# Eighteen matmuls on zeros ahead of the first scores of a fused attention and MoE kernel

## The chip, the core and the metric

The kernel runs on one core of a Trainium2 chip. The metric is the device time of one execution in microseconds (us), as the median of the runs shown. Engines are called PE (TensorE's matmuls), PEld (TensorE's weight loads, which overlap PE), DVE (VectorE), ACT (ScalarE), POOL (GpSimd) and SP (the queue that issues most DMAs).

## The reference, cut to what matters

Three stages follow each other. The output of the first is the input of the second, and so on.

```python
scores = scale * np.matmul(q, k.transpose(0, 1, 3, 2))          # B 2, H 8, S 576, D 64, causal
cum    = np.cumsum(np.maximum(s, 0.0), axis=-1)
bias   = -(cum[:, :, :, None] - cum[:, :, None, :])
attn   = softmax(np.where(causal, -1e9, scores + np.minimum(bias, 0.0)))
x      = attn @ v                                               # 1152 tokens x 512
x      = sum(p[:, e:e+1] * (np.maximum(x @ w1[e], 0) @ w2[e]) for e in range(4))
out    = np.maximum(x @ w_in, 0)**2 @ w_out                     # d_ff 2048
```

The 18 matmuls of the change read a tile of zeros and write a PSUM bank that nothing reads, so they compute no part of this.

## The kernel before, in words

**Attention.** The work is cut into 16 + 24 + 40 steps: one step is one tile of queries of one head against all its keys. The loop at L683 is a software pipeline over the steps: in its round n the scores of step n are computed on PE (`do_qk`, L415), the row minima of step n-1 on DVE (`do_scores`, L449), the exponentials of step n-2 on ACT (`do_exp`, L472), the sums and the scaling of step n-3 on DVE and POOL (`do_sums`, L482; `do_norm`, L488), the transposes of step n-4 on PE (`do_transpose`, L501) and their copies out of PSUM on ACT (`do_pt`, L525). `do_pv` (L544) then multiplies by v on PE.

**The first 16 steps** are "plain" groups of two heads (L279). Their scores are three products in one PSUM tile: q times k in full float32 (L420) and two products (L430) that add the cumulative sums, with the rows of one head (64 of 128 partitions). They need q and k (loaded into `raw_p`, L323) and `cum_k`, `cum_q` (L612 to L618). From step 16 on the scores are two products with 128 rows (L439, L440), whose second operand is put together from a copy made by DMA (`tl<-th`, L363).

**Other work beside it.** The weights of the first expert are loaded (`w_load`, L88) and split into a high and a low part by ACT and DVE (`w_split`, L110, with the copy at L114 and the subtraction at L78) in the rounds of `SPLIT_AT`. The probabilities of the experts are normed by `p_norm` (L632 to L637), which the program writes in round 12. From round 21 on (`X_AT`), parts of the first expert's matmuls (L196, L222) fill PE between the steps; they use the PSUM pool `ph` of two banks.

**What sets the order.** SP's queue keeps the order of the program (L61). The order on PE, ACT, DVE and POOL is fixed when the program is built, by a planner that goes through a simulated timeline (L1156): an engine that would stand idle in that timeline takes what is ready, even if the program writes it later. `tc.issue_after` and `pin` hold single instructions back. On the chip each engine then works through its own list in that order.

**Behind the attention** come the remaining experts and the last stage (L935 and L953 above all), which fill most of the span.

Of the kernel before, what the change touches and what calls it, by code (L numbers as in the profile page):

```python
# [8 lines left out]
F32 = mybir.dt.float32  # L9
F32R = mybir.dt.float32r  # L10
# [6 lines left out]
P = 128  # L17
# [11 lines left out]
SPLIT_AT = [*range(0, 16, 2), *range(22, 38, 2)]  # L29
NP = 5  # L30
X_AT = 21, 45
KMAX = 512


# [12 lines left out]
def fused_kernel(ctx, tc, qk, v, s, dp, w1, w2, wi, wo, out):  # L47
# [5 lines left out]
    nc = tc.nc  # L53
# [131 lines left out]
    def ph_tile():  # L185
        pool = ph_pools[ph_count[0] % len(ph_pools)]
        ph_count[0] += 1
        return pool.tile([P, 512], F32, tag="ph", name="ph")
# [111 lines left out]
    with tc.tile_pool(name="att", bufs=2) as att, tc.tile_pool(name="atc", bufs=1) as const_a:  # L300
        aps = psum.enter_context(tc.tile_pool(name="aps", bufs=1, space=PSUM))

        mask = const_a.tile([P, KMAX + P], F32, name="mask")
        nc.gpsimd.memset(mask, 0.0)
        nc.gpsimd.affine_select(
            out=mask[:, KMAX:],
            in_=mask[:, KMAX:],
            pattern=[[-1, P]],
# [4 lines left out]
        )  # L313
        y_slots[:] = [ph_p]
        h_pools[:] = [att, 256, NF]
        st_pools[:] = [att, WBUF, "raw_w"]

        def qk_load(g):
# [16 lines left out]
        def bc_load(g):  # L335
            if g.plain:
                return
            r0 = g.b * H + g.heads[0]
            nc.sync.dma_start(out=g.th[AQ, : g.nq].bitcast(F32), in_=aug_d[0, r0, :, g.q0 : g.q1])
            nc.sync.dma_start(out=g.tl[AK, S : S + g.nk].bitcast(F32), in_=aug_d[1, r0, :, : g.nk])  # L340
# [13 lines left out]
        def qk_split(g):  # L354

            if g.plain:
                return []
            raw, th, tl = g.raw, g.th, g.tl
            q, k = slice(0, g.nq), slice(S, S + g.nk)

            def high_q():
                nc.scalar.copy(th[64:, q], raw[64:, q])
                nc.sync.dma_start(out=tl[:64, q].bitcast(F32), in_=th[64:, q].bitcast(F32))  # L363

            return [
                high_q,
                lambda: nc.scalar.copy(th[:, k], raw[:, k]),
                lambda: less(nc.vector, tl[64:, q], raw[64:, q], th[64:, q]),
                lambda: less(nc.gpsimd, tl[64:, k], raw[64:, k], th[64:, k]),
            ]  # L370
# [9 lines left out]
        def v_load(b, hp, nj):  # L380
            kt, full, half = v_parts(b, nj)
            t = att.tile([P, 5, 2 * D], F32, tag="v", name="v", bufs=2)
            c = slice(hp * 2 * D, (hp + 1) * 2 * D)
            nc.sync.dma_start(
                out=t[:, full[0] : full[-1] + 1, :],
                in_=v[b, kt[full[0]] : kt[full[-1] + 1], c].rearrange("(j p) c -> p j c", p=P),
            )
            for j in half:
                nc.sync.dma_start(out=t[:64, j, :], in_=v[b, kt[j] : kt[j + 1], c])
            vt[b, hp] = t  # L390
# [6 lines left out]
        for u in units:  # L397
            for i in u.tiles:
                t = Step()
# [8 lines left out]
        i = 0  # L408
# [6 lines left out]
        def do_qk(t):  # L415
            u, g = t.u, t.u.group
            if g.plain:
                ps = aps.tile([P, 512], F32, tag="s", name="s", bufs=3)
                rows = slice(u.slot * D, (u.slot + 1) * D)
                nc.tensor.matmul(  # L420
                    ps[: t.n, : t.w],
                    lhsT=g.raw[rows, t.q0 : t.q0 + t.n],
                    rhs=g.raw[rows, g.nq : g.nq + t.w],
                    start=True,
                    stop=False,
                )
                one = pick[rows, u.h // 2, :]
                sums = ((one[:, : t.n], cum_k[rows, : t.w]), (cum_q[rows, t.q0 : t.q0 + t.n], one[:, : t.w]))
                for i, (lhs, rhs) in enumerate(sums):
                    nc.tensor.matmul(ps[: t.n, : t.w], lhsT=lhs, rhs=rhs, start=False, stop=(i == 1))  # L430
                t.ps = [(ps, 0, t.w)]
                return
            q = slice(t.q0 - g.q0, t.q0 - g.q0 + t.n)
            t.ps = []
            cuts = [(0, t.w)] if t.w <= 512 else [(0, 288), (288, 576)]
            for a, z in cuts:
                ps = aps.tile([P, 512], F32, tag="s", name="s", bufs=3)
                k = slice(S + a, S + z)
                nc.tensor.matmul(ps[: t.n, : z - a], lhsT=g.tl[:, q], rhs=g.th[:, k], start=True, stop=False)  # L439
                t.mm = nc.tensor.matmul(  # L440
                    ps[: t.n, : z - a], lhsT=g.th[:, q], rhs=g.tl[:, k], start=False, stop=True
                )
                t.ps.append((ps, a, z))

        def do_bias(t):
            m0 = KMAX + t.n - t.w
            t.bias = mask[: t.n, m0 : KMAX + t.n]

# [33 lines left out]
        def do_sums(ts):  # L482
            t, c = ts[0], ts[0].c
            n, m = t.n, len(ts)
            nc.vector.tensor_scalar(t.st[:n, 4 + c : 4 + c + m], t.st[:n, 4 + c : 4 + c + m], 1e-9, None, op0=ALU.add)
            nc.vector.reciprocal(t.st[:n, 6 + c : 6 + c + m], t.st[:n, 4 + c : 4 + c + m])  # L486

        def do_norm(t):  # L488
            nc.gpsimd.tensor_scalar(  # L489
                t.p[: t.n, : t.w], t.p[: t.n, : t.w], t.st[: t.n, 6 + t.c : 7 + t.c], 1.0, op0=ALU.mult, op1=ALU.mult  # L490
            )
# [147 lines left out]
        def v_args(gi):  # L639
            g = groups[gi]  # L640
            return g.b, g.heads[0] // 2, 2 if gi < 4 else 5
# [8 lines left out]
        def w_ahead(n):  # L650
            while wloaded[0] < min(wdone[0] + n, len(PIECES)):
                w_load(0, *PIECES[wloaded[0]])
                wloaded[0] += 1
# [29 lines left out]
        for n in range(nsteps + 8):  # L683

            def step(i):
                return steps[i] if 0 <= i < nsteps else None

            cur, s1, s2, s3, s4, s5 = (step(n - i) for i in range(6))
            gi = group_first.get(n)
            if gi is not None:  # L690
                if gi + 1 < len(groups):
                    if gi > 0:
                        split_ops = qk_split(groups[gi + 1])
                        bc_load(groups[gi + 1])
                if gi > 0 and groups[gi].heads[0] % 2 == 0:
                    v_load(*v_args(gi))
            if s5 is not None:
                do_pt(s5)

            if s3 is not None and (s3.mate is None or s3.c == 1):  # L700
                ts = [s3] if s3.mate is None else [s3.mate, s3]
                do_sums(ts)
                for t in ts:
                    do_norm(t)

            if cur is not None:
                do_qk(cur)
            if pending_pv:
                x_next = pending_pv.pop(0)
                do_pv(x_next)  # L710
            if s4 is not None:
                do_transpose(s4)
            if s5 is not None and s5.last:
                u = s5.u
                if u.h % 2:
                    pending_pv.append(u)
                else:
                    pair[u.b, u.q0, u.h] = u

            if n + 1 < nsteps:  # L720
                do_bias(steps[n + 1])
            if s1 is not None:
                do_scores(s1)
            if s2 is not None:
                do_exp(s2)
            if x_next is not None:
                do_x(x_next)
            x_next = None
            nxt = min((i for i in group_first if i > n), default=n + 1) - n
            if gi is None:  # L730
                for _ in range(-(-len(split_ops) // nxt)):
                    split_ops.pop(0)()
            if n + 1 in group_first and 4 <= group_first[n + 1] + 2 < len(groups):
                qk_load(groups[group_first[n + 1] + 2])
            if n >= SPLIT_AT[0] - 4:
                w_ahead(WBUF)
            if n in SPLIT_AT:
                w_step()
            if n == 12:
                p_norm()  # L740
            if n == X_AT[0]:
                fill = fill_of((0, 256))
                rate = sum(c for _, c in fill) / (X_AT[1] - X_AT[0])
            elif n == X_AT[1]:
                fill += fill_of((256, 256))
                rate = sum(c for _, c in fill) / (nsteps + 2 - X_AT[1])
            owed += rate
            while fill and owed > 0:
                part, cost = fill.pop(0)
                with tc.issue_after(steps[min(n, nsteps - 1)].mm.ins):  # L750
                    part()
                owed -= cost
# [407 lines left out]
```

## Time and profile before

| | |
|---|---|
| runs shown | 718.12 us median of 3 (717.85, 718.12, 720.88) |
| the profiled execution | 719.2 us, its span 717.4 us |
| PE, PEld, DVE, ACT, POOL busy, share of the span | 96%, 83%, 71%, 49%, 43% |
| mean granted TensorE clock over the span | 0.996 |

The span goes from the first to the last instruction; the remaining 1.8 us lie around it. A matmul's busy time in the profile includes the time in which it drains, so matmuls that follow each other overlap in these rows, and the distance from one start to the next tells more than the length of one. "Granted clock" is a share of TensorE's full speed of 2.4 GHz: 1.00 is the upper of its two levels, 0.50 the lower.

### The profile page before, as it was taken

The page shows a single profiled execution, that of the slowest core. Times are in us where ns is not written, and L with a number is a line of the kernel's source. Part 1 is how long each engine was busy: PE and PEld are TensorE (multiplying, and loading weights), DVE is VectorE, ACT ScalarE, POOL GpSimd, SP SyncE. Part 2 cuts the span into 40 slices and gives each one's busy share as a digit, 9 for nine tenths or more (in the row PEclk, how much of TensorE's full clock was granted, in tenths as well). Part 3 has the DMA queues.
Part 4 walks back from the last instruction along what each step waited for, and adds up shares of the span by engine and source line. Part 5 has one row for each costly group of instructions (what it writes and reads, how often), then busy time and mean ns, then how long its engine had stood idle before and what let it go on. Part 6 is the DMA issues. An engine that isn't in the chain of part 4 may idle for free.

```text
span 717.4 us, 11852 instructions
## 1 busy us (share of the span) xinstructions
PE 689.6 (96%) x4100; PEld 598.5 (83%) x4100; DVE 507.6 (71%) x1145; ACT 353.1 (49%) x881; POOL 311.9 (43%) x332
## 2 busy tenths in 40 slices
PE   4999999999999999999999999999999999999997
PEld 3678788778998998989989989889997888899996
DVE  6668667762378548787787787869587788955463
ACT  4789767752254453443342534335474445535341
POOL 4446534431043675292580852822528625704000
PEclk9999999999999999999999999999999999999999
DMA  4554333200121234344242443441203232210012
GB/s 139 169 162 148 93 85 84 62 25 1 60 84 64 89 114 136 108 136 139 85 165 90 148 147 105 132 121 70 60 22 111 77 122 96 89 30 1 1 59 73
DMA packets 37179, 66.37 MB, mean 93 GB/s; under 512 B 4512, under 2 KB 12208, under 8 KB 37120
## 3 DMA queue, kind: packets, MB, share of 16 engines
q1 hardware_dynamic: 27904, 40.45, 18.7%
q10 hardware_dynamic: 9216, 25.17, 10.7%
q8 instruction: 32, 0.52, 0.3%
q14 instruction: 27, 0.22, 0.1%
HBM read 52.87 MB, written 10.90 MB: 89 GB/s over the span
## 4 chain that ended last, share of the span: by engine, by line
PE 74%; DVE 12%; ACT 4%; issue 4%; DMA 2%; POOL 2%; SPq 1%; ACTq 0%; DVEq 0%; POOLq 0%
PE y L953 26%; PE ph L935 17%; PE pc L935 7%; PE ph L196 7%; PE y L222 6%; PE o L560 4%; PE pt L512 3%; DVE dy L144 2%; PE s L439 2%; DVE raw_d L148 2%; PE s L440 1%; DVE raw_d L140 1%; ACT p L473 1%; POOL w L78 1%; DVE h L988 1%
## 5 line engine op out<-in xcount | busy, mean ns | idle before, releaser
L953 PE MATMUL y<-w,h 128*128 128x512 f32 x1080 | 276.7, 393 | 0.7 <-ACT h L993 0.7
L953 PEld LDWEIGHTS y<-w,h 128*128 128x128 f32 x1080 | 194.2, 188 | 32.0 <-ACT h L993 0.9
L935 PE MATMUL ph<-tx,w 128*128 128x256 f32 (+1 forms) x720 | 116.2, 297 | 0.1
L935 PEld LDWEIGHTS ph<-tx,w 128*128 128x128 f32 x720 | 106.9, 190 | 7.6 <-ACT u L976 0.9
L976 ACT COPY u<-ph 128x256 f32<-128x256 f32 (+1 forms) x120 | 47.7, 397 | 96.1 <-PE ph L935 93.9
L78 POOL TENSOR_TENSOR w<-raw_w,w 128x512 fp32r<-128x512 f32 x58 | 79.4, 1383 | 21.5 <-ACT w L902 21.5
L935 PE MATMUL pc<-xh,w 128*128 128x256 f32 (+1 forms) x320 | 78.2, 299 | 6.2 <-DVE r L992 2.8
L935 PE MATMUL ph<-xh,w 128*128 128x256 f32 (+1 forms) x320 | 78.3, 299 | 1.7 <-DVE h L988 1.2
L489 POOL TENSOR_SCALAR p<-p,stat 128x128 f32<-128x128 f32 (+8 forms) x80 | 46.8, 597 | 72.8 <-DVE stat L486 30.4
L78 POOL TENSOR_TENSOR w<-val,w 128x512 fp32r<-128x512 f32 x40 | 58.6, 1480 | 43.4 <-PE ph L196 41.7
L133 POOL TENSOR_SCALAR dy<-dy 128x512 f32<-128x512 f32 x32 | 20.0, 626 | 116.1 <-ACT dy L131 108.7
L935 PEld LDWEIGHTS pc<-xh,w 128*128 128x128 f32 x320 | 55.9, 188 | 10.4 <-DVE h L988 3.8
L935 PEld LDWEIGHTS ph<-xh,w 128*128 128x128 f32 x320 | 56.1, 189 | 5.1 <-DVE h L988 1.9
L473 ACT ACTIVATE p<-p,stat 128x128 f32<-128x128 f32 (+8 forms) x80 | 46.6, 583 | 23.7 <-DVE stat L459 20.3
L222 PE MATMUL y<-w,h 128*128 128x512 f32 x216 | 57.7, 396 | 0.0
L196 PE MATMUL ph<-xh,w 128*128 128x256 f32 (+1 forms) x256 | 57.3, 299 | 0.1
L459 DVE CUSTOM_DVE_ANT_0 p<-s,mask 128x128 f32<-128x128 f32 (+8 forms) x80 | 35.8, 451 | 17.7 <-PE pt L512 8.8
L935 PE MATMUL ph<-xl,w 128*128 128x256 f32 (+1 forms) x160 | 47.5, 297 | 0.0
L935 PE MATMUL pc<-xl,w 128*128 128x256 f32 (+1 forms) x160 | 47.3, 296 | 0.0
L994 DVE TENSOR_TENSOR h<-r,h 128x256 fp32r<-128x256 f32 (+1 forms) x64 | 36.2, 571 | 13.7 <-ACT h L993 12.5
L196 PEld LDWEIGHTS ph<-xh,w 128*128 128x128 f32 x256 | 43.1, 188 | 1.5 <-DVE h L210 0.4
L222 PEld LDWEIGHTS y<-w,h 128*128 128x128 f32 x216 | 38.7, 188 | 6.2 <-DVE stat L459 0.3
(135 smaller groups left out, 1272.7 us busy)
## 6 DMA issues: line engine op xcount, KB each, us to landing
raw_w<-in_w SPq DMA_DIRECT2D x64, 256.0 KB
raw_d<-in_wi ACTq DMA_DIRECT2D x16, 512.0 KB
staged<-dy ACTq DMA_DIRECT2D x32, 256.0 KB
raw_d<-in_wo ACTq DMA_DIRECT2D x16, 512.0 KB
raw_w<-staged SPq DMA_DIRECT2D x32, 256.0 KB
raw<-in_qk SPq DMA_DIRECT2D x40, 144.0 KB
v<-in_v SPq DMA_DIRECT2D x8, 256.0 KB
out<-acc_a SPq DMA_DIRECT2D x6, 256.0 KB
```

Source lines behind the costliest of these rows:

```text
L78: eng.tensor_tensor(out_, a, b.bitcast(F32), op=ALU.subtract)
L196: nc.tensor.matmul(ps[:, :n], lhsT=w1_ap(e, wh, kk, f), rhs=x[:, kk, t0 : t0 + n], start=(i == 0), stop=(i == 3 * KD - 1),)
L222: mm = nc.tensor.matmul(ps, lhsT=h[:, hh, o : o + P], rhs=w2_ap(e, wh, f), start=(f == 0 and i == 0), stop=(f == NF - 1 and i == 2),)
L459: nc.vector.tensor_tensor_reduce(t.p[: t.n, a:z], ps[: t.n, : z - a], t.bias[:, a:z], scale=-0.125, scalar=init, op0=ALU.add, op1=ALU.min, ...
L473: nc.scalar.activation(t.p[: t.n, : t.w], t.p[: t.n, : t.w], AF.Exp, bias=t.nmax, scale=-1.0, accum_out=t.st[: t.n, 4 + t.c : 5 + t.c],)
L489: nc.gpsimd.tensor_scalar(t.p[: t.n, : t.w], t.p[: t.n, : t.w], t.st[: t.n, 6 + t.c : 7 + t.c], 1.0, op0=ALU.mult, op1=ALU.mult)
L512: nc.tensor.transpose(tp_ap(t, j), t.p[: t.n, kt[j] : kt[j + 1]], ident[: t.n, : t.n])
L560: return nc.tensor.matmul(u.o[i * D : (i + 1) * D, qs - u.q0 : u.nq], lhsT=vv[:kn, j, i * D : (i + 1) * D], rhs=rhs, start=(j == 0), stop= ...
L935: nc.tensor.matmul(ps[:, :n], lhsT=pw[q][s][:, wh, c : c + P], rhs=x_part(b, xn, xx, k2), start=(first and m == 0), stop=(m == 5), skip_gr ...
L953: nc.tensor.matmul(ps, lhsT=hs[j][:, hh, o : o + P], rhs=wt[e, 2, g][:, wh, j * DM : (j + 1) * DM], start=(g % 2 == 0 and i == 0 and j == ...
L976: nc.scalar.copy(t[:, :n], ps[:, :n])
L994: nc.vector.tensor_tensor(lo, r, hi.bitcast(F32), op=ALU.subtract)
```

## The change

A tile of zeros is set by DVE, one tile of the pool `ph` is taken and never read, and 18 matmuls of 128 rows, 128 columns of weights and 512 columns of data, all zeros, write it. They stand in the program ahead of the attention's loads and steps. `WARM` also has places for more such matmuls behind the scores of the first rounds; with its last number 0 none is issued there.

```diff
+WARM = 18, 0, 0
...
         h_pools[:] = [att, 256, NF]
+        zeros = const_a.tile([P, 512], F32R, name="zeros")
+        nc.vector.memset(zeros.bitcast(F32), 0.0)
+
+        def keep_warm(after, n):
+            with tc.issue_after(after) if after is not None else nullcontext():
+                for _ in range(n):
+                    nc.tensor.matmul(idle, lhsT=zeros[:, :P], rhs=zeros, start=True, stop=True)
+
+        idle = ph_tile()
+        keep_warm(None, WARM[0])
         st_pools[:] = [att, WBUF, "raw_w"]
...
-                    nc.tensor.matmul(ps[: t.n, : t.w], lhsT=lhs, rhs=rhs, start=False, stop=(i == 1))
+                    t.mm = nc.tensor.matmul(ps[: t.n, : t.w], lhsT=lhs, rhs=rhs, start=False, stop=(i == 1))
...
             if cur is not None:
                 do_qk(cur)
+                if n < WARM[2]:
+                    keep_warm(cur.mm.ins, WARM[1])
```

## Rows read from the trace of the kernel before

**Rows 1.** Busy us of each engine by stretch, then granted clock, DMA share, GB/s
```profile
12.65:34.30 21.65, 20.77 (x83) 14.63 (x83) 15.40 (x54) 16.60 (x53) 9.66 (x14) 1.00 0.57 168
...
12.65:43.80 31.15, 28.09 (x111) 19.25 (x111) 21.57 (x76) 23.45 (x72) 12.84 (x20) 1.00 0.54 162
...
46.60:60.00 13.40, 13.40 (x106) 12.08 (x106) 10.48 (x37) 12.41 (x32) 9.76 (x10) 1.00 0.61 181
```

**Rows 2.** PE by shape, 8 to 36.2 us: count, busy us, mean ns, idle before
```profile
L512 PE MATMUL pt<-ident,p 128*128 128x128 f32 x18 | 6.1, 443 | 0.6 <-ACT ptk L536 0.5
```

**Rows 3.** The same view, 43 to 110 us
```profile
L512 PE MATMUL pt<-ident,p 128*128 128x128 f32 x68 | 11.3, 276 | 1.0 <-POOL p L489 1.0
```

**Rows 4.** PE in order of time, 36 to 45 us: start, length, instruction
```profile
36.30 0.66 PE L439 MATMUL s<-th,tl 128*128 128x384 f32 x1 [1.06 <-DMA tl<-th]
...
37.07 0.63 PE L439 MATMUL s<-th,tl 128*128 128x512 f32 x1
37.50 0.63 PE L440 MATMUL s<-tl,th 128*128 128x512 f32 x1
...
41.20 0.94 PE L512 MATMUL pt<-ident,p 128*128 128x128 f32 x3
43.10 0.55 PE L512 MATMUL pt<-ident,p 128*128 128x128 f32 x3 [0.96 <-POOL p L489]
...
44.28 0.39 PE L439 MATMUL s<-th,tl 128*128 128x512 f32 x1
44.51 0.40 PE L440 MATMUL s<-tl,th 128*128 128x512 f32 x1
```

**Rows 5.** PE in order of time, 538 to 562 us
```profile
541.59 1.04 PE L935 MATMUL ph<-tx,w 128*128 128x320 f32 x6
...
545.52 0.42 PE L935 MATMUL pc<-xh,w 128*128 128x320 f32 x1 [1.23 <-DVE u L983]
...
547.05 0.41 PE L935 MATMUL ph<-xh,w 128*128 128x320 f32 x1 [0.38 <-DVE r L992]
...
548.36 1.80 PE L935 MATMUL ph<-tx,w 128*128 128x320 f32 x6
```

**Rows 6.** Busy us by stretches of 1 us, as in rows 1
```profile
548.00:549.00 1.00, 1.00 (x6) 1.00 (x5) 0.69 (x2) 1.00 (x3) 0.56 (x1) 0.50 0.79 266
...
551.00:552.00 1.00, 1.00 (x7) 0.83 (x6) 0.87 (x3) 0.65 (x2) 1.00 (x2) 0.98 0.61 84
```

**Rows 7.** PE in order of time, 463 to 476 us
```profile
471.48 0.39 PE L935 MATMUL ph<-xh,w 128*128 128x256 f32 x1 [1.18 <-DVE h L988]
```

**Rows 8.** Busy us by stretches of 5 us, as in rows 1
```profile
470.00:475.00 5.00, 3.82 (x21) 3.05 (x20) 4.02 (x9) 1.45 (x4) 0.08 (x1) 1.00 0.39 122
```

**Rows 9.** All engines in order of time, 0 to 16 us
```profile
0.79 0.06 DVE L63 MEMSET warm<- 1x1 f32 x1 [0.79 <-PEq L1150]
0.86 0.64 POOL L304 MEMSET mask<- 128x640 f32 x1
...
2.53 1.02 DVE L593 TENSOR_SCALAR sc<-sc 16x320 f32<-16x320 f32 x1 [1.69 <-DMA sc<-in_s]
...
7.85 1.65 PE L420 MATMUL s<-raw_p 64*128 64x128 f32 x6 [7.85 <-DMA raw_p<-in_qk]
...
9.61 0.78 PE L430 MATMUL s<-w,cum_q 64*128 64x128 f32 x3
10.24 0.75 DVE L628 TENSOR_SCALAR aug<-aug 16x1152 fp32r<-16x1152 f32 x1
...
12.17 0.19 DVE L634 TENSOR_REDUCE psum__364<-praw 128x9 f32<-128x36 f32 x1 [1.18 <-DMA praw<-in_dp]
12.30 0.29 DVE L459 CUSTOM_DVE_ANT_0 p<-s,mask 128x128 f32<-128x128 f32 x1
...
12.65 1.22 PE L420 MATMUL s<-raw_p 64*128 64x256 f32 x3 [2.25 <-DVE stat L459]
...
15.31 0.60 ACT L114 CAST w<-raw_w 128x512 fp32r<-128x512 f32 x1
...
15.95 0.69 DVE L78 TENSOR_TENSOR w<-raw_w,w 128x512 fp32r<-128x512 f32 x1
```

## The prediction, made before the result was known

> **What bounds the kernel now.** I read the busy times by stretch first. From 46.6 us on PE is the bound: it is busy 13.40 us of 13.40 right there [rows 1]. PE's later work is the same before and after, so whatever the change is worth must come from PE's reaching that state earlier or later. Its place is the start, up to about 44 us.
>
> Second, the same shapes at two places. In the first stage a transpose of 128x128 takes 443 ns [rows 2], later 276 ns [rows 3]; two matmuls of 512 columns start 0.43 us apart at 37.07 us, and 0.23 us apart at 44.28 us [rows 4]. So TensorE runs at its lower level (1.2 GHz) up to some 42 us and at the upper (2.4 GHz) from 43.10 us, where three transposes take 0.55 us instead of 0.94 [rows 4]. The granted-clock column says 1.00 for the early stretches too [rows 1]; there the lengths contradict it, and I go by the lengths. The clock rose after PE had worked without a gap since 36.30 us [rows 4]. It had not risen before, though PE was busy 20.77 us of the 21.65 between 12.65 and 34.3 [rows 1].
>
> Third, the start in order of time [rows 9]. PE does nothing until q and k land at 7.85 us. Its first scores are done at 9.61 + 0.78 = 10.39 us. They then wait: DVE finishes L628 at 10.99, stands in front of the norming of probabilities (L634) until their load lands, and takes the first scores at 12.30. PE's next scores, released by that, start at 12.65 after 2.25 us of idleness.
>
> **The zeros' tile.** DVE's new memset has 128x512 elements. The nearest price is POOL's memset of 128x640, 0.64 us; in the same proportion 0.51, and DVE's 0.69 us for a 128x512 subtraction is the upper end [rows 9]. DVE is idle from 0.85 to 2.53 us for a load, so it costs nothing there. Without that cover it would cost its 0.5 to 0.7 us. PE can then start at about 0.85 + 0.6 = 1.45 us. No DMA is added, and SP, ACT and POOL get no new instruction. The unread bank belongs to a pool that the program uses only from round 21 on; until then no one waits for it.
>
> **The eighteen matmuls.** All at the lower level: 18 x 0.43 = 7.74 us [rows 4], with some 0.2 us for the last to drain, and so an end at 1.45 + 7.94 = 9.39 us, 1.54 us behind the landing of q and k. If the clock rises on the way, they end earlier: all at the upper level is 18 x 0.23 = 4.14 us and an end at 5.8 us. These are the two ends. PE's own record of a rise is the one after 36.30 us, within about 6 us of steady work [rows 4]; at 548.36 us the lower level gave way within 3 us of dense work [rows 5, 6]. Either puts the rise inside the burst, so I take an end between 7 and 8.8 us.
>
> **What the first scores gain or lose.** They take 10.39 - 7.85 = 2.54 us at the lower level. In the worst case they start at 9.24, when the last zeros have streamed, and end at 11.8 us. In the best they start at 7.85 and take 0.23/0.43 of that, 1.4 us, to end at 9.2 us. Both lie ahead of 12.30 us, where DVE takes them. So 0 us on the path, with 0.5 us left in the worst case; what covers them is DVE's wait for the probabilities. If that wait were gone, DVE could take them at 10.99: the worst case would then cost 0.8 us against a start at that time, and the best nothing.
>
> **Is the clock still up at 12.65?** This decides. The trace shows one fall: PE stood idle 1.23 us, did six matmuls, stood 0.38 us, and then the granted clock was 0.50 from 548 to 551 us; six matmuls that had taken 1.04 us took 1.80 [rows 5, 6]. It shows a hold as well: after 1.18 us of idleness at 470 us, with dense work on both sides, the clock stayed at 1.00 [rows 7, 8]. In the changed kernel there lies between the zeros' end and 12.65 us a wait of at least 2.25 us [rows 9], up to 3.4 if the scores run fast (12.65 - 9.2), and beside it only scores on half the rows. That is more idleness than the fall had, and less work around it. I take it that the clock is at 1.2 GHz again at about 12.65 us. From there to 42 us the stage is that of before, and of that the trace says that its work, even with PE 96% busy, doesn't raise the clock [rows 1]. Gain: 0 us; if the clock outlasts the gap by 2 us or so, the scores and transposes up to 15 us gain at most half of that, 1 us.
>
> **Sum.** 0 (memset) + 0 (first scores) + 0 (clock, 0 to -1) = 0 on a profiled execution of 719.2 us (span 717.4 and 1.8 around it). That execution lies 1.1 us above the median of the runs, 718.1 us, to which the forecast is tied: 718.0 us.
>
> **Rival 1, faster: the clock stays up through the first stage.** For it: a hold over 1.18 us of idleness is in the trace [rows 7, 8], and PE is the fullest engine from 12.65 to 43.80 us, 28.09 of 31.15 us, so the stage would shorten [rows 1]. Against it: the one fall had a shorter wait than the one here [rows 5, 6]. Price: at full clock PE needs 28.09 x 0.23/0.43 = 15 us, so ACT with 23.45 us becomes the bound; at the share that ACT reaches in the next stage, 12.41/13.40 = 0.93, the stage takes 25.3 us instead of 31.15: -5.8 us, 712.2 us. The waits for DMA copies that stay would take part of it back; 2 us is the low end. The Trainium skill, TensorE: Matmul & The Clock Gate, section "Why this matters for your kernels", advises to issue matmuls ahead of the timed work, and puts the fall down to idle gaps longer than the 2.25 us here. By that rule the clock would hold at 10.39 to 12.65 us, and this rival would be the forecast. The trace's fall after 1.23 us doesn't agree with it.
>
> **Rival 2, slower: the planner turns the order on DVE.** The zeros stand ahead of the scores in the planner's timeline too, which makes DVE seem idle longer. It fills such holes with later work: the norming that the program writes in round 12 already stands ahead of the first scores [rows 9]. If one subtraction of a split weight (L78) came ahead of L459 as well, DVE would wait for the weights and ACT's copy: L78 ran from 15.95 to 16.64 us, so the first scores would be taken at 16.64 instead of 12.30 [rows 9]. Price +4.3 us, 722.4 us, less what the later steps catch up (ACT is busy only 16.60 of 21.65 us there [rows 1]), so +2 to +4.3. It decides from the first split that is placed there. Against it: the weights' loads stand behind those of the probabilities on SP, so the planner should see them late as well.
>
> **Rival 3: the zeros don't raise the clock at all.** No row shows a burst on zeros. The burst then takes 7.74 us, the first scores end at 11.8 us and are still covered: 718.1 us. In time this can't be told from the forecast.
>
> **How the numbers follow.** Forecast (rise, then fall before or soon after 12.65) 0.52, rival 3 0.15, rival 1 0.17, rival 2 0.16. About 0.5%, 3.6 us, is what a measurement of this kernel can tell from no change; the three runs of before span 3 us. Rival 1's price lies beyond it for most of its bounds, as does rival 2's at its full price; a shorter rival 2 counts as no change, and in return a plan that is turned in another place can also cost. So faster 0.17, same 0.67, slower 0.16. The range holds both cases without change with their scatter up to 720.9, rival 1 down to two thirds of its price (718.0 - 4 = 714.0) and rival 2 up to 721.8, short of its full price. Left out are the ends of both rivals, together under 0.2.
>
> **What the changed profile would show.** The zeros on PE from about 1.5 us, first 0.43 us apart and then 0.23. The first scores between 7.85 and 9.3 us; L459 at about 12.3. Transposes between 12.65 and 42 us of about 443 ns again, and three transposes of 0.55 us only behind some 43 us. I am wrong if the transposes at 13 to 30 us take 276 ns (rival 1), if a subtraction L78 stands ahead of the first L459 on DVE (rival 2), or if PE's first gap-free work of L196 starts more than 2 us away from 46.6 us.

## The result, and the profile after

Behind the change the median is 723.32 us (20 runs, 720.59 to 726.25), beside 718.35 us for the kernel before (20 runs, 715.49 to 720.93): ratio 1.0069, 95% interval 1.0052 to 1.0085. It is slower by 5 us, where 718.0 was forecast. A second set of runs (e6 below) gave 1.0042 [1.0022, 1.0062]. The profiled execution is the quickest of its 20: 720.59 us, span 718.8, mean clock 0.979; so its trace shows less of the loss than the median does. Its lines are those of before plus 1 near the top and plus 13 further down: L420, L459, L512 and L196 are now L433, L472, L525 and L197.

The start, all engines in order of time, of the kernel after (start, length, instruction, in brackets the idle time before it and what ended it):

```profile
0.94 0.48 DVE L318 MEMSET zeros<- 128x512 f32 x1
...
1.48 6.20 PE L325 MATMUL ph<-zeros 128*128 128x512 f32 x18 [1.48 <-DVE zeros L318]
...
7.83 0.92 PE L433 MATMUL s<-raw_p 64*128 64x128 f32 x6 [0.17 <-DMA raw_p<-in_qk]
...
9.11 0.49 PE L443 MATMUL s<-w,cum_q 64*128 64x128 f32 x3
...
11.88 0.19 DVE L647 TENSOR_REDUCE psum__385<-praw 128x9 f32<-128x36 f32 x1 [1.39 <-DMA praw<-in_dp]
12.11 0.17 DVE L648 TENSOR_SCALAR psum__385<-psum__385 128x9 f32<-128x9 f32 x1
12.31 0.22 DVE L649 RECIPROCAL psum__385<-psum__385 128x9 f32<-128x9 f32 x1
12.44 0.29 DVE L472 CUSTOM_DVE_ANT_0 p<-s,mask 128x128 f32<-128x128 f32 x1
...
12.80 0.79 PE L433 MATMUL s<-raw_p 64*128 64x256 f32 x1 [3.19 <-DVE stat L472]
```

Against [rows 9]: the first scores are done at 9.60 instead of 10.39 us, DVE takes them at 12.44 instead of 12.30, and PE's wait grows from 2.25 to 3.19 us. So the zeros have bought idle time here and nothing else. The busy times by stretch (columns as in [rows 1]) show what the clock did with that:

```profile
5.40:7.70 2.30, 2.27 (x10) 1.50 (x8) 1.77 (x4) 1.54 (x3) 1.27 (x3) 1.00 0.71 189
...
12.65:34.30 21.65, 21.20 (x83) 15.62 (x84) 11.90 (x52) 15.87 (x51) 8.83 (x16) 0.50 0.49 158
12.65:43.80 31.15, 28.04 (x108) 20.00 (x108) 18.60 (x74) 22.26 (x70) 11.09 (x19) 0.51 0.49 153
46.60:60.00 13.40, 13.35 (x103) 11.86 (x103) 12.02 (x39) 12.38 (x31) 8.46 (x10) 1.00 0.60 177
```

The upper level comes inside the burst, at 5.39 us, and is gone at 12.22, in PE's wait. From there to 42.94 us the column reads 0.50, with transposes of 446 ns as before [rows 2]; behind 43 us they take 278 ns [rows 3]:

```profile
L525 PE MATMUL pt<-ident,p 128*128 128x128 f32 x16 | 5.5, 446 | 0.0
...
L525 PE MATMUL pt<-ident,p 128*128 128x128 f32 x68 | 11.0, 278 | 0.8 <-POOL p L502 0.4 <-ACT ptk L549 0.3
```

All that is as forecast. But look at DVE in the stretch to 34.30: 11.90 us of work where it had 15.40 [rows 1]. DVE does other work there. **The order has changed.** SP's queue is the same; the lists of PE, DVE and ACT differ from those of before in some 50 places each, POOL's in a few. The first difference is on DVE at 12.11 us: two more instructions of the norming (L648, L649, shown above) stand ahead of the first row minimum, where before one stood [rows 9]. On PE it begins at about 15 us (two more sets of scores ahead of the first transposes). In the trace the last differences are at about 125 us on PE and 130 us on DVE; behind them nothing differs. Two places show what it does. PE near 37 us, in order of time:

```profile
36.94 0.66 PE L452 MATMUL s<-th,tl 128*128 128x384 f32 x1 [2.03 <-DMA tl<-th]
37.40 0.53 PE L453 MATMUL s<-tl,th 128*128 128x384 f32 x1
37.72 0.63 PE L452 MATMUL s<-th,tl 128*128 128x512 f32 x1
38.14 0.63 PE L453 MATMUL s<-tl,th 128*128 128x512 f32 x1
38.57 0.45 PE L452 MATMUL s<-th,tl 128*64 128x288 f32 x1
38.81 0.45 PE L453 MATMUL s<-tl,th 128*64 128x288 f32 x1
39.05 0.84 PE L525 MATMUL pt<-ident,p 128*128 128x128 f32 x3
```

Before, the wait for the copy `tl<-th` was 1.06 us [rows 4], and behind two sets of scores came a transpose. In the kernel before, PE's next two lines are:

```profile
37.93 0.41 PE L512 MATMUL pt<-ident,p 128*128 128x128 f32 x1
37.99 0.59 PE L439 MATMUL s<-th,tl 128*64 128x288 f32 x1
```

Now three transposes stand behind three sets of scores and a longer wait; the scores themselves begin 0.64 us later. And PE near 131 us, in the kernel after:

```profile
128.74 0.86 PE L223 MATMUL y<-w,h 128*128 128x512 f32 x3
131.33 0.63 PE L525 MATMUL pt<-ident,p 128*64 128x128 f32 x4 [1.73 <-POOL p L502]
```

The same instruction in the kernel before:

```profile
129.33 0.62 PE L512 MATMUL pt<-ident,p 128*64 128x128 f32 x4 [0.65 <-POOL p L489]
```

That is 1.08 us more of waiting. The order on DVE just ahead of it points to where it comes from. DVE and POOL in the kernel after:

```profile
127.74 1.45 DVE L79 TENSOR_TENSOR tl<-raw,th 64x576 fp32r<-64x576 f32 x1 [0.48 <-ACT th L375]
...
129.61 0.47 DVE L472 CUSTOM_DVE_ANT_0 p<-s,mask 128x320 f32<-128x320 f32 x1
...
130.01 0.15 DVE L499 RECIPROCAL stat<-stat 64x1 f32<-64x1 f32 x1
...
130.36 2.55 POOL L502 TENSOR_SCALAR p<-p,stat 64x64 f32<-64x64 f32 x5 [1.79 <-DVE stat L498]
```

In the kernel before:

```profile
126.15 1.33 DVE L78 TENSOR_TENSOR tl<-raw,th 64x576 fp32r<-64x576 f32 x1
...
128.00 0.15 DVE L486 RECIPROCAL stat<-stat 64x1 f32<-64x1 f32 x1
...
128.36 1.64 POOL L489 TENSOR_SCALAR p<-p,stat 64x64 f32<-64x64 f32 x3 [1.50 <-DVE stat L485]
128.38 0.49 DVE L459 CUSTOM_DVE_ANT_0 p<-s,mask 128x320 f32<-128x320 f32 x1
```

In the new order DVE's subtraction waits 0.48 us for ACT's cast, and a row minimum of 0.47 us stands ahead of the reciprocal that POOL's scaling needs. Together that is most of the 1.08 us; neither was tried alone.

The row minimum of step 16 comes 2.41 us later than before (39.83 against 37.42), the first L197 1.38 us (48.04 against 46.66), and L950 begins 2.08 us later (212.46 against L935's 210.39). At the end of the spans 1.4 us are left of that. The order behind is the same, but the clock is not: in the execution of before it was at the lower level from 547.62 to 551.03 us as well, in that of after it wasn't.

### The profile page after: what moved, and what is told of

Its sections match the earlier page's. It is cut to its first block, busy times and chain, and to the rows that moved or that the text cites. A ratio compares the mean times of both kernels' runs of the same rounds, so it can differ in the third digit from the quotient of the medians.

```text
span 718.8 us, 11889 instructions
## 1 busy us (share of the span) xinstructions
PE 694.5 (97%) x4118; PEld 602.1 (84%) x4118; DVE 504.7 (70%) x1146; ACT 353.0 (49%) x881; POOL 310.4 (43%) x332
## 4 chain that ended last, share of the span: by engine, by line
PE 76%; DVE 12%; issue 4%; ACT 3%; POOL 2%; SPq 1%; DMA 1%; ACTq 1%; DVEq 0%; POOLq 0%
PE y L968 26%; PE ph L950 16%; PE pc L950 7%; PE ph L197 7%; PE y L223 6%; PE o L573 4%; PE pt L525 4%; DVE dy L145 2%; PE s L452 2%; DVE raw_d L149 2%; PE s L453 1%; DVE raw_d L141 1%; PE s L433 1%; POOL w L79 1%; DVE h L1003 1%
## 5 line engine op out<-in xcount | busy, mean ns | idle before, releaser
L950 PE MATMUL ph<-tx,w 128*128 128x256 f32 (+1 forms) x720 | 115.5, 296 | 0.1
L950 PEld LDWEIGHTS ph<-tx,w 128*128 128x128 f32 x720 | 106.2, 189 | 7.5 <-ACT u L991 0.9
L79 POOL TENSOR_TENSOR w<-raw_w,w 128x512 fp32r<-128x512 f32 x58 | 80.2, 1398 | 20.2 <-ACT w L917 20.2
L950 PE MATMUL pc<-xh,w 128*128 128x256 f32 (+1 forms) x320 | 78.4, 299 | 6.6 <-DVE r L1007 3.1
L950 PE MATMUL ph<-xh,w 128*128 128x256 f32 (+1 forms) x320 | 78.0, 298 | 1.7 <-DVE h L1003 0.8
L79 POOL TENSOR_TENSOR w<-val,w 128x512 fp32r<-128x512 f32 x40 | 58.6, 1480 | 43.6 <-ACT w L910 43.6
L502 POOL TENSOR_SCALAR p<-p,stat 128x128 f32<-128x128 f32 (+8 forms) x80 | 45.3, 580 | 69.6 <-DVE stat L499 42.6
L950 PEld LDWEIGHTS pc<-xh,w 128*128 128x128 f32 x320 | 56.0, 188 | 11.2 <-DVE r L1007 4.4
L950 PEld LDWEIGHTS ph<-xh,w 128*128 128x128 f32 x320 | 56.0, 188 | 5.1 <-DVE h L1003 1.5
L197 PE MATMUL ph<-xh,w 128*128 128x256 f32 (+1 forms) x256 | 58.0, 301 | 0.1
L472 DVE CUSTOM_DVE_ANT_0 p<-s,mask 128x128 f32<-128x128 f32 (+8 forms) x80 | 35.6, 452 | 25.2 <-PE pt L525 20.2
L950 PE MATMUL ph<-xl,w 128*128 128x256 f32 (+1 forms) x160 | 47.4, 296 | 0.0
L950 PE MATMUL pc<-xl,w 128*128 128x256 f32 (+1 forms) x160 | 47.4, 296 | 0.0
L197 PEld LDWEIGHTS ph<-xh,w 128*128 128x128 f32 x256 | 43.1, 188 | 1.4 <-DVE h L211 0.4
```

The source lines that it names most:

```text
L79: eng.tensor_tensor(out_, a, b.bitcast(F32), op=ALU.subtract)
L197: nc.tensor.matmul(ps[:, :n], lhsT=w1_ap(e, wh, kk, f), rhs=x[:, kk, t0 : t0 + n], start=(i == 0), stop=(i == 3 * KD - 1),)
L472: nc.vector.tensor_tensor_reduce(t.p[: t.n, a:z], ps[: t.n, : z - a], t.bias[:, a:z], scale=-0.125, scalar=init, op0=ALU.add, op1=ALU.min, ...
L502: nc.gpsimd.tensor_scalar(t.p[: t.n, : t.w], t.p[: t.n, : t.w], t.st[: t.n, 6 + t.c : 7 + t.c], 1.0, op0=ALU.mult, op1=ALU.mult)
L950: nc.tensor.matmul(ps[:, :n], lhsT=pw[q][s][:, wh, c : c + P], rhs=x_part(b, xn, xx, k2), start=(first and m == 0), stop=(m == 5), skip_gr ...
```

## The experiments

Medians of the kernel before in these sets: 720.11 us for e1 to e4, 719.04 for e5 to e8, 719.11 for e9 to e12, 719.51 for e13 to e16. Every kernel here computes the whole result; zeros and order are all that differs.

**First question: the clock and the zeros, or the order?** One to ten zeros leave the order on every engine as before; from 11 on the planner gives another, and 11, 15 and 18 each give their own.

e1, ten zeros:

```diff
-WARM = 18, 0, 0
+WARM = 10, 0, 0
```

> Ten zeros instead of eighteen. All engines keep the order of the kernel before; only the memset and the ten matmuls are new. Theory P (the new order of instructions that the planner makes in the attention costs the time): as before, ratio 0.998 to 1.002, about 718.3 us. Theory C (the clock's early rise and fall costs the time, by a later second rise): the clock rises at about 5 us here too and falls again before 13, so +3 to +5 us, ratio 1.004 to 1.007.

717.84 us against 720.11: ratio 0.9977 [0.9958, 0.9996]. With the order of before, ten zeros do no harm. Stretches of its profile (columns as in [rows 1]):

```profile
34.30:37.00 2.70, 2.70 (x10) 2.10 (x10) 2.00 (x11) 1.70 (x7) 0.97 (x3) 0.50 0.74 225
37.10:46.60 9.50, 7.29 (x56) 5.23 (x54) 7.31 (x25) 8.69 (x24) 5.24 (x7) 1.00 0.56 162
```

Its second rise came at 37.05 us, where the kernel before had it at 42.45, and its L197 began 1.77 us earlier than before. But its row minimum of step 16 came at 36.23 us, 1.20 us early, and that is ahead of the rise. The last section says how far executions scatter here.

e2 has 11 zeros (`WARM = 11, 0, 0`), the first number that turns the order:

> Eleven zeros: one more than the run with ten, but the planner now orders PE, ACT, DVE and POOL in another way from the first steps on. P: it has a time of its own, over 2 us away from the run with ten, to either side. C: the same as the run with ten within 1 us, since 0.2 to 0.4 us of zeros more change nothing in the clock.

719.51 us, 1.0000 [0.9982, 1.0018]: 1.7 us above e1, less than the theory of the order asked for, and no loss against before.

e3 has 15 (`WARM = 15, 0, 0`), with a third order:

> Fifteen zeros, a third order. P: a time of its own between 716 and 725 us, not in line with the number of zeros. C: as the changed kernel, about +5 us (723).

720.21 us, 1.0004 [0.9989, 1.0019]. So an order that differs doesn't have to cost; the one for 18 zeros does.

e4 keeps the count at 18 and takes half of the array's columns:

```diff
-                    nc.tensor.matmul(idle, lhsT=zeros[:, :P], rhs=zeros, start=True, stop=True)
+                    nc.tensor.matmul(idle[:64], lhsT=zeros[:, :64], rhs=zeros, start=True, stop=True)
```

> Eighteen zeros with 64 columns of weights instead of 128: half the array. The order of PE, ACT and POOL is that of the changed kernel (one instruction on DVE two places earlier). I expect that the half array doesn't raise the clock, so that the zeros run at the lower level up to about 9.4 us and are still covered. P: slower like the changed kernel, +3 to +6 us, ratio 1.005 to 1.008, though the clock has not risen early. C: as before, 718.3 us, ratio 0.998 to 1.002.

722.86 us, 1.0042 [1.0022, 1.0062]. It was meant to take the clock's rise away and leave the order. The rise stayed: the clock rose at 4.97 us and fell at 11.80, as a stretch of its profile shows. The time is that of the changed kernel, and nothing was told apart.

```profile
5.00:9.00 4.00, 3.52 (x19) 1.87 (x17) 3.33 (x6) 2.18 (x4) 1.51 (x3) 1.00 0.71 178
```

**Second question: one instruction, or the whole order?** In the kernel after, a weight's subtraction (L79, at 39.02 us) stands ahead of step 16's row minimum on DVE. DVE there, in order of time:

```profile
39.02 0.69 DVE L79 TENSOR_TENSOR w<-raw_w,w 128x512 fp32r<-128x512 f32 x1 [1.07 <-ACT w L115]
39.83 0.56 DVE L472 CUSTOM_DVE_ANT_0 p<-s,mask 128x384 f32<-128x384 f32 x1
```

e5 moves that one subtraction behind the row minimum:

```diff
-                nc.vector.tensor_tensor_reduce(
+                t.sc = nc.vector.tensor_tensor_reduce(
...
-                w_step()
+                with tc.issue_after(steps[17].sc.ins) if n == 24 else nullcontext():
+                    w_step()
```

> The changed kernel with one instruction moved: the subtraction of the tenth weight piece on DVE is held back behind the row minima of step 17; every other instruction of every engine stands as in the changed kernel. P (the new order costs the time, and this subtraction in front of the row minima of step 16 is its main piece): the minima of step 16 start at about 38 us instead of 39.8 and 1 to 2 us of the loss come back, ratio to the changed kernel about 0.998. Rival (the loss lies in the order as a whole or in the clock): no change against the changed kernel.

722.38 us, 1.0043 [1.0025, 1.0061], beside e6, the changed kernel again:

> The changed kernel itself, unchanged, beside the others on one chip. P and C: ratio to before 1.005 to 1.008. If on this chip it is below 1.003, half of the measured loss was the chip's.

722.47 us, 1.0042 [1.0022, 1.0062], less than the 1.005 to 1.008 expected of it. The subtraction is not the cause. DVE in e5 shows what the row minimum waits for without it:

```profile
37.59 0.17 DVE L499 RECIPROCAL stat<-stat 128x2 f32<-128x2 f32 x1
39.64 0.56 DVE L472 CUSTOM_DVE_ANT_0 p<-s,mask 128x384 f32<-128x384 f32 x1 [1.88 <-PE pt L525]
```

It waits for the transposes: it writes a buffer `p` that they must have read, and on PE they now stand behind three sets of scores that wait for a copy.

**Third question: what is it worth to hold the clock?** e7 and e8 use the change's own places for more zeros, three behind each of the first 16 steps' scores; the planner turns the order in both.

```diff
-WARM = 18, 0, 0
+WARM = 10, 3, 16
```

> Ten zeros ahead and three behind the scores of each of the first 16 steps: does the clock stay at 2.4 GHz through the first stage, and is that worth the 2 to 5.8 us that I priced it at? If it stays up: transposes of about 276 ns between 13 and 34 us, and the first L196 2 to 5 us earlier, 713 to 716 us. If the zeros' own time (48 x 0.23 = 11 us of PE) eats it, as before, 717 to 720. If the clock falls all the same, 48 x 0.43 = 21 us of PE at the lower level and over 5 us slower.

741.13 us, median of six, of which five lie between 739.93 and 743.02 and one at 719.99. In the profile, of the run at 743.02, the clock is low from 8.17 to 62.78 us, and L197 begins 24.3 us late. The run at 719.99 may have kept its clock, but it has no trace, and its mean of 0.999 doesn't tell: a run of 741.67 reads 0.996. The profile's stretch, PE busy throughout and still at 1.2 GHz:

```profile
8.20:62.70 54.50, 54.50 (x150) 34.87 (x147) 19.86 (x69) 20.30 (x60) 9.67 (x16) 0.50 0.34 97
```

e8 has `WARM = 18, 3, 16`:

> The same with eighteen zeros ahead, and with yet another order on all engines. If the clock is what counts (C): as the run with ten and three within 1 us. If the order counts (P): apart from it by more than 1 us.

724.41 us, 1.0064 [1.0040, 1.0088]. Here the clock was up from 4.31 to 134 us, as its stretch shows, and yet L197 began 2.7 us late.

```profile
12.65:34.30 21.65, 21.20 (x104) 14.76 (x104) 12.90 (x50) 14.40 (x44) 7.38 (x13) 1.00 0.51 150
```

**Fourth question: zeros and order apart.** `replay` ties each instruction on PE, DVE, ACT and POOL to the one ahead of it in a list written into the kernel, without a semaphore, so that the planner has no choice left. e9 has all 18 zeros and the list of the kernel before:

```diff
         fused_kernel(tc, *args, out)
+        replay(nc, tc)
...
+        for prev, ins in zip(want, want[1:]):
+            tc.add_manual_dep(
+                ins,
+                prev.name,
+                mybir.DependencyInfo(mybir.DependencyClass.NoSync, mybir.DependencyReason.DATA),
+                reason="replay",
+            )
```

> The changed kernel, all eighteen zeros, with every engine held to the order of the kernel before (zeros first on PE, their memset second on DVE). P (the new order costs the time, the zeros nothing): ratio to before 0.996 to 1.002, as the run with ten zeros. C (clock or zeros): as the changed kernel, 1.004 to 1.007.

719.15 against 719.11 us: 1.0001 [0.9984, 1.0018]. The zeros cost nothing and gain nothing. PE in e9 near 130 us, with the short wait of before:

```profile
129.81 0.63 PE L525 MATMUL pt<-ident,p 128*64 128x128 f32 x4 [0.66 <-POOL p L502]
```

e10 is the kernel before, without a zero, held to the changed kernel's list (the same diff on the kernel before):

> The kernel before, no zeros at all, with every engine held to the order of the changed kernel. P: slower like the changed kernel, ratio 1.004 to 1.007, with PE waiting 1.7 us for POOL's scaling at about 131 us. C: as before, 0.998 to 1.002.

723.8 us, 1.0075 [1.0048, 1.0101]. **The order alone costs what the change costs.** PE in e10:

```profile
133.29 0.63 PE L512 MATMUL pt<-ident,p 128*64 128x128 f32 x4 [1.73 <-POOL p L489]
```

e11 and e12 hold the clock in the order of before: 18 zeros ahead, and one or two behind each of the first 16 steps' scores (`WARM = 18, 1, 16` and `18, 2, 16`, with `replay`).

> Eighteen zeros ahead and one behind the scores of each of the first 16 steps, everything else held to the order of the kernel before. Does the clock stay up without a new order, and what is that worth? If it stays up, rival 1's price of the prediction is tested: -2 to -5.8 us (0.992 to 0.997). If it falls, the 16 zeros cost up to 16 x 0.43 = 7 us.

730.35 us, 1.0167 [1.0139, 1.0194]: the clock fell at 12.74 and came back at 46.87 us, so 16 zeros were paid at the lower level and L197 began 8.15 us late.

> The same with two zeros behind each step's scores. If one zero doesn't hold the clock and two do: 0.992 to 0.998. The zeros' own time at the upper level is 32 x 0.23 = 7.4 us of PE, which before was the fullest engine of the stage, so the gain is smaller than with one if both hold it.

717.17 us, 0.9977 [0.9960, 0.9995]. The clock was up from 4.47 to 42.02 us, as the stretch shows; L197 began 1.09 us earlier than before.

```profile
12.65:34.30 21.65, 21.65 (x112) 14.63 (x111) 15.05 (x51) 16.74 (x53) 9.19 (x14) 1.00 0.54 169
```

e1 and e12 are quicker than both kernels, by 1.6 us in 720, close to what can be told.

**Fifth question: which part of the order?** With all 18 zeros and `replay`, the list is spliced: up to PE's 167th matmul behind the zeros (about 50 us) or its 418th (about 85 us) from the one kernel, the rest from the other. e13 is new, then old:

> All 18 zeros; every engine follows the order of the changed kernel up to TensorE's 167th matmul behind the zeros (about 50 us), and the order of the kernel before from there. Theory A (the cost lies in the first 50 us, where three sets of scores stand ahead of transposes near 37 us): the cost is all here, ratio to before 1.004 to 1.006, L197 at least 1 us later than before. Theory B (the cost lies in the order behind 50 us, seen as the longer wait for GpSimd's scaling at 131 us): ratio 1.000 +- 0.0015. Theory C (each part costs some): 1.002 to 1.003.

721.11 against 719.51 us: 1.0027 [1.0009, 1.0045].

> All 18 zeros; the reverse: order of the kernel before up to TensorE's 167th matmul (about 50 us), order of the changed kernel from there. Theory A: ratio to before 1.000 +- 0.0015. Theory B: 1.004 to 1.006, with the wait of 1.7 us at some 131 us. Theory C: 1.002 to 1.003.

720.80 us: 1.0021 [1.0002, 1.0040]. The same pair with the splice at 85 us:

> All 18 zeros; order of the changed kernel up to TensorE's 418th matmul (about 85 us), then that of the kernel before. Theory A: as e13, 1.004 to 1.006. Theory B: 1.000 if what costs stands between 85 and 115 us, else 1.004. Theory C: between.

721.37 us: 1.0036 [1.0016, 1.0055].

> All 18 zeros; order of the kernel before up to TensorE's 418th matmul (about 85 us), then that of the changed kernel, whose last difference lies near 115 us. Theory A: 1.000 +- 0.0015. Theory B: 1.004 with the wait of 1.7 us at 131 us if the differences at 85 to 115 us make it, else 1.000. Theory C: 1.001 to 1.002.

720.33 us: 1.0015 [0.9994, 1.0037]. The medians say that each part costs some: 0.27% + 0.21% and 0.36% + 0.15% both give about 0.5%, where the whole was 0.42% (e6) to 0.75% (e10). The first part measured larger both times, but the intervals overlap, and that of e16 takes in no loss at all, so which part is larger isn't shown. The traces separate without overlap. The table gives starts, as differences in us to the profiled execution of before; step 16 is the 17th row minimum, "131 us" is PE's wait for POOL there, and the last column is by how much the stretch between the 71st and the 91st row minimum (124.51 and 156.18 us before) grew:

| order to 50 us / from 85 us | step 16 | first L197 | wait at 131 us | growth behind it |
|---|---|---|---|---|
| before | 0 (37.42) | 0 (46.66) | 0.65 | 0 |
| e1, old / old | -1.20 | -1.77 | 0.65 | -0.03 |
| e9, old / old | +0.23 | +0.49 | 0.66 | -0.02 |
| e14, old / new | -0.72 | -1.04 | 1.73 | +2.64 |
| e16, old / new | -1.37 | -2.06 | 1.73 | +2.64 |
| e13, new / old | +1.84 | +3.43 | 0.65 | -0.03 |
| e15, new / old | +1.66 | +2.34 | 0.65 | +0.09 |
| after | +2.41 | +1.38 | 1.73 | +1.17 |
| e4, new / new | +2.25 | +1.11 | 1.75 | +1.21 |
| e5, new / new | +2.21 | +1.32 | 1.73 | +1.17 |
| e6, new / new | +2.19 | +1.34 | 1.73 | +2.74 |
| e10, new / new | +2.47 | +3.47 | 1.73 | +3.12 |

The wait of 1.73 us (1.75 in e4) is there with every new list behind 85 us and with no other in the table. It adds 1.08 us by itself. The rest is the clock, as stretches of e16 show:

```profile
34.30:37.20 2.90, 2.90 (x10) 2.14 (x10) 2.12 (x12) 1.75 (x7) 0.93 (x3) 0.50 0.86 234
37.30:46.60 9.30, 7.41 (x55) 5.49 (x55) 6.95 (x26) 8.92 (x25) 5.39 (x8) 1.00 0.55 156
128.00:129.40 1.40, 1.32 (x10) 0.67 (x12) 0.76 (x3) 0.00 (x0) 1.40 (x4) 1.00 0.19 74
129.50:132.80 3.30, 3.30 (x18) 2.59 (x17) 0.63 (x3) 2.17 (x6) 0.14 (x1) 0.50 0.00 0
```

PE in e16 stood idle for 1.73 us up to 128.07 us, and from 129.41 to 132.83 the clock was at its lower level; in e6 it was so from 132.22 to 135.63, and in e10 and e14 too. In the profiles of after, e4 and e5 the same wait brought no fall: growth 1.17 to 1.21 instead of 2.64 to 3.12. The fall is thus worth 1.4 us and more, and comes in some executions. In e9, e13 and e15, with a wait of some 0.65 us, there is none.

The early part holds such falls too. In e13 PE waited 1.73 us near 43 us for ACT to copy transposes out of PSUM (`ptk`), and from 42.84 to 49.67 us the clock was at its lower level:

```profile
42.92 0.66 PE L525 MATMUL pt<-ident,p 128*128 128x128 f32 x2 [1.73 <-ACT ptk L549]
```

```profile
42.90:49.60 6.70, 6.49 (x28) 4.39 (x28) 3.54 (x13) 4.34 (x11) 3.51 (x4) 0.50 0.51 141
```

In e10 and e15 the same wait was 1.15 and 1.34 us, with falls at 45.47 and 43.96 us; in e6 it was 1.68 us without a fall. So L197's delay of 2.34 to 3.47 us in these three has a fall in it; 1.11 to 1.38 us, in after, e4, e5 and e6, is the delay without one.

The Trainium skill, TensorE: Matmul & The Clock Gate, section "Why this matters for your kernels", puts the fall down to idle gaps longer than any of these. Near 131 us a gap of 1.73 us was followed by one in four profiles out of seven (e6, e10, e14, e16; not after, e4, e5), and the measurement decides; by the page's rule the last column would read about +1.2 in all seven.

## Why the prediction was wrong

**Right, step by step.** The memset took 0.48 us, a little under the 0.51 to 0.69 given, in DVE's idle time. The burst ended at 7.68 us (7 to 8.8). The first scores were covered. (Their worst case should begin at 9.19 us by its own terms, 1.45 + 7.74, instead of 9.24; nothing hangs on it.) The clock was at 1.2 GHz again ahead of the next scores, after 3.19 us of idleness (up to 3.4 was allowed for), and transposes took 446 ns. Rival 3 is out: zeros do raise the clock. By e9, all of these steps together are worth 1.0001 [0.9984, 1.0018], and the sum of 0 that was made for them holds.

**The step that failed** is "From there to 42 us the stage is that of before", and with it "PE's later work is the same before and after". It is the same stage only if its order is, and the text had said itself that the planner goes through a simulated timeline in which the zeros stand too. The term that was missing is the new order, costed at 0 and worth 3 to 5 us (e6, e10). The prediction looked for a turned order in one place, a subtraction ahead of the first row minimum (rival 2), found an argument against that place, and gave "a plan that is turned in another place" no price of its own: it was set off against the short end of rival 2. Rival 2 was right in kind and wrong in place: no L79 stands ahead of the first L472, only two short instructions of the norming, and it starts at 12.44 instead of 12.30 us. By the traces, what costs is transposes behind scores near 37 us and a longer wait at 131 us, in some executions with a clock fall behind either. In the traces of the splices either part of the list delays the work. Which single instruction does it is not shown; the subtraction moved in e5 doesn't.

The test "L196 more than 2 us away from 46.6" would not have found it in this profile: 48.04 us. The stretch that was read as untouched, the later attention, holds the rest.

**Rival 1** (2 to 5.8 us for a clock that stays up) was not priced by these runs. In e12 the clock was held to 42 us and L197 came 1.09 us earlier, the median 1.9 us lower, but with 32 more zeros on PE; in e8 it was held in another order and the kernel lost. In e12 the row minimum of step 15 came at 35.10 us where it had been at 35.22: the steps still came at the old pace, and the gain arose behind it. The row of e12 leaves PE no room: it is busy for 21.65 of 21.65 us. Counted from each start to the next, its zeros take 7.95 us of that stretch and its other work 13.70, where that work had taken 20.77 [rows 1]. So on PE the zeros that held the clock used up what it gave. What a held clock would give without them was not tried, and the price stays open.

**Chances.** Slower had 0.16. The 723.32 us lie outside the range, which ended at 721.8; that end was a part of rival 2's price, and nothing behind 50 us was in it.

## What to carry to other kernels

Where a planner orders the engines, a few added instructions can edit the whole order (here 11 did, 10 did not): compare the order on every engine before a term is put at zero, and hold it fixed to learn what the edit itself is worth. Ask what the real work behind matmuls that raise the clock waits for: here the first scores ended 0.79 us sooner, and the gap behind them was 0.94 us longer. And a wait on PE of 1 to 2 us can cost twice, once for itself and, in some executions, once for the clock behind it.

## What the runs showed that was not expected

- **The rise scatters.** e9, e14 and e16 have the same zeros and the same list to 50 us, and their second rise came at 42.38, 38.69 and 37.25 us; L197 began at 47.15, 45.62 and 44.60. That is 2.5 us between executions of the same instructions, and some of the gain of e1 (rise at 37.05) may be no more than that. Not all of it is the clock: the row minimum of step 16 was 1.6 us apart (37.65 to 36.05) ahead of these rises. The first rise scatters too: in eleven profiles that begin with the same 18 zeros it came between 4.31 (e8) and 6.53 us (e16). The Trainium skill, TensorE: Matmul & The Clock Gate, section "What's actually happening", says that the point of the rise varies from run to run, by half a microsecond either way. These runs agree that it varies, by over 1 us either way.
- **The clock rose on half the array too.** Zeros on 64 columns of weights raised the clock at 4.97 us (e4), those on 128 at 5.39 (after) and 4.83 (e9).
- **PE's records are full at either level.** In the profile of e7 they fill 54.50 of 54.50 us at 0.50; in e12 they fill 21.65 of 21.65 at 1.00. With one zero behind each step the clock fell (e11), with two it stayed up to 42.02 us (e12). Why is not shown.
- **The column needs a first event.** In the kernel before it read 1.00 up to 42 us [rows 1], where the lengths say 1.2 GHz. With zeros the same stretch reads 0.50. Nothing is recorded ahead of the first change of level (at 42.45 us in the kernel before), and the column then shows the upper one.
